# Grouped-query attention on one core: Q pieces copied four times by GpSimd for full-width transposes, and Q loaded by another pattern

## The chip, the cores and the metric

The kernel runs on one core of one Trainium2 chip. The metric is the device time of one execution in microseconds (us), as a median over several runs; the profile is of one more execution. The core has five engines with instruction streams of their own: PE (TensorE: matmuls and, on a second row of the profile called PEld, the loading of their weights), DVE (VectorE), ACT (ScalarE), POOL (GpSimd) and SP (SyncE, which here only issues DMAs). Sixteen DMA engines move data between HBM and the on-chip memory SBUF. PE writes its results to another on-chip memory, PSUM, in which DVE and ACT read them.

## The reference

```python
B, Hq, Hkv, Sq, Sk, D = 16, 32, 8, 16, 2048, 128      # all bf16
k = jnp.repeat(k, rep, axis=1)                         # rep = Hq // Hkv = 4
v = jnp.repeat(v, rep, axis=1)
scores = jnp.einsum("bhqd,bhkd->bhqk", q, k) * D ** -0.5
p = softmax(scores, axis=-1)
out = jnp.einsum("bhqk,bhkd->bhqd", p, v)
```

There are 16 x 8 = 128 groups (one batch, one KV head). A group has 4 x 16 = 64 rows of Q, and 2048 x 128 of K and of V, 512 KB each. K and V together are 134 MB; Q and the output are 2.1 MB each.

## The kernel before, in words

**Tiling.** Two groups make a *pair*: 128 rows of Q, and so 128 rows of scores. There are 64 pairs, p = 0 to 63. K and V of a pair are loaded whole (1 MB each; six buffers Kn, eight buffers Vb). Eight pairs make a *chunk* c of Q: 1024 rows, 256 KB, loaded at once into Qn (two buffers), eight rows side by side in each of 128 partitions.

**One pair.** DVE transposes K in blocks of 32x32 four-byte words, two bf16 at a time (line 261, Kn to KT). Since a word holds two neighbouring elements of D and only 32 words fit in a block's side, the head dimension of 128 falls into four pieces of 32 (numbered by b and e), and the keys into four strips of 32 partitions. S (line 217): 32 matmuls, 4 pieces x 4 strips x 2 groups, each with 32 rows contracted, add the scores up in PSUM. DVE scales and negates them and keeps the minimum (line 277, Sneg). ACT takes the exponential and the row sums (line 306, P). PE transposes P in two halves of four 128x128 blocks (line 232, "PT"), and ACT moves each half to SBUF (line 316, "pe"). PV (line 243): 32 matmuls with V into O_ps. ACT scales by the reciprocal of the row sum (line 326, "norm"), and SP stores the 32 KB of the pair (line 166).

**Q.** S needs Q transposed: for each of the four pieces, 32 elements of D on the partitions, and the same 32 again on each of the four strips of 32 partitions. A *part* (c, i), i = 2b + e, makes one piece for the 1024 rows of a chunk. At line 200 PE transposes, for each of the 8 rows j of a partition, the 32 columns of the piece (every second element of 64) four times, once into each strip r: 32 transposes a part, 32 parts in all. ACT then moves the part, 128x1024, from PSUM to QT (line 296), with j taken innermost, so that the rows come out in their order.

**Order.** The order on PE and on ACT is written out by hand in two lists. First the four parts of chunk 0 and S(0). Then for each p: PE has S(p+1), a part of the next chunk if p mod 8 is 2 to 5, PT(p) in two halves, PV(p); ACT has exp(p), norm(p-1), the part's move, the two halves. PE's transposes go through three stages of PSUM in turn, and each waits until ACT has emptied its stage. DVE has Sneg(p), the reciprocal of p-1 and the two K transposes of p+2.

**SP's queue.** For t = 0, 1, ...: load K(t); load a chunk c of Q where t = max(0, 8c-7); load V(t-3); store pair t-7. Each waits in that one queue: K for DVE's transposes of the buffer's last user, V for PV of its last user (line 152), a store for the norm of its pair (line 165), and from chunk 2 on Q for the transposes of the chunk two before (line 159). Every load adds 16 to its semaphore, one from each of the 16 DMA engines, and its reader waits for all 16.

**GpSimd** makes the two identity matrices for the transposes (lines 132 to 135) and nothing else.

Of the kernel before, what the change touches and what calls it, by code (L numbers as in the profile page):

```python
# [5 lines left out]
ACT = mybir.ActivationFunctionType  # L6
ALU = mybir.AluOpType
BF16 = mybir.dt.bfloat16
# [8 lines left out]
NQ = 2  # L17
# [6 lines left out]
def bass_standalone__gqa_softmax__sampling_kernel(  # L24
# [14 lines left out]
    NQC = NP // 8  # L39
# [3 lines left out]
    sb = lambda name, shape, dt: ctx.enter_context(nc.sbuf_tensor(name, shape, dt))  # L43
    sem = lambda name: ctx.enter_context(nc.semaphore(name))

    iota_t = sb("iota_t", [128, 128], I32)
    ident = sb("ident", [128, 128], BF16)
# [5 lines left out]

    KT = [sb(f"KT{i}", [128, 2, J * 64], F32) for i in range(NKT)]
    Qn = [sb(f"Qn{i}", [128, 8, 128], BF16) for i in range(NQ)]

    QT = [sb(f"QT{i}", [128, 4, 1024], BF16) for i in range(2)]
    Sneg = [sb(f"Sneg{i}", [128, Sk], F32) for i in range(2)]
    P = [sb(f"P{i}", [128, Sk // 2], F32) for i in range(2)]
# [14 lines left out]
    sem_q = [sem(f"sem_q{i}") for i in range(NQ)]  # L74
    sem_o = [sem(f"sem_o{i}") for i in range(NO)]
    sem_kt = sem("sem_kt")
    sem_max = sem("sem_max")
    sem_rec = sem("sem_rec")
    sem_s = sem("sem_s")
    sem_st = sem("sem_st")  # L80
# [5 lines left out]
    qf = q.rearrange("b h s d -> (b h s) d")  # L86
# [8 lines left out]
    def stage(*what):  # L95
        stages.append(what)
        return len(stages) - 1
# [9 lines left out]
    for p in range(NP):  # L107
# [5 lines left out]
        c, i = divmod(p, 8)  # L113
        if c + 1 < NQC and 2 <= i < 6:
            q_part(c + 1, i - 2)
        for h in range(2):
            u = stage("P", p, h)
# [4 lines left out]
    last_q = {what[1:]: u for u, what in enumerate(stages) if what[0] == "Q"}  # L122
    last_p = {what[1:]: u for u, what in enumerate(stages) if what[0] == "P"}

    def stage_ap(u):
        return ST_ps[:, 512 * (u % NSTAGE):512 * (u % NSTAGE + 1)]

    with nc.Block() as block:

        @block.gpsimd  # L130
        def _(gp):
            gp.iota(iota_t[:, :], [[1, 128]], base=0, channel_multiplier=-1).then_inc(sem_id, 1)  # L132
            gp.wait_ge(sem_id, 1)
            gp.tensor_scalar(ident[:, :], iota_t[:, :], 0.0, None, op0=ALU.is_equal).then_inc(sem_id, 1)  # L134
            gp.tensor_scalar(ident4[:, :], iota_t[:, :], 0.0, None, op0=ALU.is_equal).then_inc(sem_id, 1)  # L135

        @block.sync
        def _(sp):
            def load_k(p):
                s = p % NK  # L140
                if p >= NK:
                    sp.wait_ge(sem_kt, 2 * (p - NK) + 2)
                if p == 0:
                    for g in range(2):
                        sp.dma_start(Kn[s][:, g, :], kf[:, g, :]).then_inc(sem_k0[g], 16)  # L145
                else:
                    sp.dma_start(Kn[s][:, :, :], kf[:, 2 * p:2 * p + 2, :]).then_inc(sem_k[s], 16)

            def load_v(p):
                s = p % NV  # L150
                if p >= NV:
                    sp.wait_ge(sem_pv, p - NV + 1)
                dst = Vb[s][:, :, :, :].rearrange("a g j d -> a g (j d)")
                sp.dma_start(dst, vf[:, 2 * p:2 * p + 2, :]).then_inc(sem_v[s], 16)

            def load_q(c):
                s = c % NQ
                if c >= NQ:
                    sp.wait_ge(sem_st, last_q[c - NQ, 3] + 1)
                src = qf[1024 * c:1024 * (c + 1), :].rearrange("(a j) d -> a j d", j=8)  # L160
                sp.dma_start(Qn[s][:, :, :], src).then_inc(sem_q[s], 16)

            def store(p):
                s = p % NO
                sp.wait_ge(sem_nm, p + 1)
                sp.dma_start(of[128 * p:128 * (p + 1), :], Osb[s][:, :]).then_inc(sem_o[s], 16)

            for t in range(NP + SLAG + 1):
                if t < NP:
                    load_k(t)  # L170
                for c in range(NQC):
                    if t == max(0, 8 * c - QLEAD):
                        load_q(c)
                if 0 <= t - VLAG < NP:
                    load_v(t - VLAG)
                if 0 <= t - SLAG < NP:
                    store(t - SLAG)
            for s in range(NO):
                sp.wait_ge(sem_o[s], 16 * (NP // NO))

        @block.tensor
        def _(pe):
            pe.wait_ge(sem_id, 3)

            def free(u):
                if u >= NSTAGE:
                    pe.wait_ge(sem_ev, u - NSTAGE + 1)

            for op in pe_prog:
                if op[0] == "QT":  # L190
                    _, c, i, u = op
                    if i == 0:
                        pe.wait_ge(sem_q[c % NQ], 16 * (c // NQ + 1))
                    free(u)
                    dst = stage_ap(u).bitcast(BF16)
                    src = Qn[c % NQ][:, :, :].rearrange("p j (b c e) -> p j b e c", b=2, e=2)
                    b, e = divmod(i, 2)
                    for j in range(8):
                        for r in range(4):
                            ins = pe.transpose(dst[32 * r:32 * (r + 1), 128 * j:128 * (j + 1)], src[:, j, b, e, :], ident[:, :])  # L200
                    ins.then_inc(sem_st, 1)
                elif op[0] == "S":
                    _, p = op
                    pe.wait_ge(sem_kt, 2 * p + 2)
                    if p >= 1:
                        pe.wait_ge(sem_max, p)
                    c, i = divmod(p, 8)
                    if i == 0:
                        pe.wait_ge(sem_ev, last_q[c, 3] + 1)
                    kt = KT[p % NKT][:, :, :].bitcast(BF16).rearrange("p g (t b x e) -> p g b e t x", t=J // 2, b=2, e=2)  # L210
                    qt = QT[c % 2]
                    for acc in range(4):
                        b, e = divmod(acc, 2)
                        for r in range(4):
                            rows = slice(32 * r, 32 * (r + 1))
                            for g in range(2):
                                ins = pe.matmul(  # L217
                                    S_ps[64 * g:64 * (g + 1), 512 * r:512 * (r + 1)],
                                    qt[rows, acc, 128 * i + 64 * g:128 * i + 64 * (g + 1)],
                                    kt[rows, g, b, e, :, :],  # L220
                                    start=(acc == 0), stop=(acc == 3),
                                )
                    ins.then_inc(sem_s, 1)
                elif op[0] == "PT":
                    _, p, h, u = op
                    if h == 0:
                        pe.wait_ge(sem_exp, p + 1)
                    free(u)
                    dst = stage_ap(u)
                    for t in range(4):  # L230
                        x = 4 * h + t
                        ins = pe.transpose(dst[:, 128 * t:128 * (t + 1)], P[p % 2][:, 128 * x:128 * (x + 1)], ident4[:, :])  # L232
                    ins.then_inc(sem_st, 1)
                elif op[0] == "PV":
                    _, p = op
                    pe.wait_ge(sem_ev, last_p[p, 1] + 1)
                    pe.wait_ge(sem_v[p % NV], 16 * (p // NV + 1))
                    if p >= 1:
                        pe.wait_ge(sem_nm, p)
                    pt = PT[p % NPT][:, :, :].bitcast(BF16).rearrange("p t (q e) -> p t e q", e=2)  # L240
                    for j in range(J):
                        for g in range(2):
                            ins = pe.matmul(  # L243
                                O_ps[64 * g:64 * (g + 1), 0:128],
                                pt[:, j // 2, j % 2, 64 * g:64 * (g + 1)],
                                Vb[p % NV][:, g, j, :],
                                start=(j == 0), stop=(j == J - 1),
                                skip_group_check=True,
                            )
                    ins.then_inc(sem_pv, 1)  # L250
# [38 lines left out]
        def _(act):  # L289
            for op in act_prog:  # L290
                if op[0] == "qe":
                    _, c, i, u = op
                    act.wait_ge(sem_st, u + 1)
                    if c >= 2 and i == 0:
                        act.wait_ge(sem_s, 8 * (c - 1))
                    act.activation(  # L296
                        QT[c % 2][:, i, :].rearrange("p (a j) -> p a j", j=8),
                        stage_ap(u).bitcast(BF16).rearrange("p (j a) -> p a j", j=8), ACT.Copy,
                    ).then_inc(sem_ev, 1)
                elif op[0] == "exp":  # L300
                    _, p = op
# [9 lines left out]
                elif op[0] == "pe":  # L311
                    _, p, h, u = op
# [7 lines left out]
                else:  # L320
                    _, p = op
# [34 lines left out]
```

## Time and profile before

| | us |
|---|---|
| median of 3 runs (lowest, highest) | 357.61 (357.51, 357.91) |
| span of the profiled execution, first to last instruction | 357.7 |
| PE busy, of that line 200 (Q transposes) | 248.2, 22.9 |
| DVE busy, of that lines 277 and 261 | 296.1, 146.1 and 150.7 |
| ACT busy, of that line 296 (Q part to QT), x32 | 249.4, 32.4 |
| POOL busy | 1.4 |
| loads of V, K: median from issue to landing | 16.0, 15.0 |
| loads of Q, x8: median from issue to landing | 14.3 |

How to read it: the profiled execution's own time is known by its span, 357.7 us. Times of the profile are counted from the span's start. A line of a group of instructions gives the busy time and the mean of one; matmuls overlap, so that the mean of one can be many times the distance between two. A line of the waits gives the engine, what it was about to do and what ended its waiting, then us in total, how many times, and the longest. A line of the timeline gives the start, the length, the engine, the source line, what was done, and in brackets the idle time before it. GpSimd's few instructions are: MEMSET of one column 98 to 101 ns, IOTA of 128 columns (int32) 234 ns, TENSOR_SCALAR of 128 columns (int32 to bf16, to f32) 534 and 526 ns.

The queues: q1 carries what SP issues, q8 and q14 carry instructions to the engines. The packets of q1 are 4 KB for K and V, 2 KB for Q and 256 bytes for the output.

### The profile page before, as it was taken

How to read it: one execution, taken by the hardware profiler on the slowest of the kernel's cores; microseconds unless marked ns; L12 is line 12 of the kernel's file. 1: busy time of each engine (PE TensorE's matmuls, PEld its weight loads, DVE VectorE, ACT ScalarE, POOL GpSimd, SP SyncE). 2: the span in 40 equal slices, each digit the busy share in tenths (PEclk: the TensorE clock that was granted, in tenths of full speed). 3: DMA queues.
4: the chain of work that ended last, by engine and by line, in shares of the span. 5: the costliest groups of instructions: out<-in, count | busy, mean ns of one | idle time of the engine just before them, and what ended most of it. 6: DMA issues, size and time to landing. Idle time of an engine off the chain costs nothing.

```text
span 357.7 us, 12753 instructions
## 1 busy us (share of the span) xinstructions
PE 248.2 (69%) x5632; PEld 171.7 (48%) x5632; DVE 296.1 (83%) x320; ACT 249.4 (70%) x353; POOL 1.4 (0%) x7
## 2 busy tenths in 40 slices
PE   2587786686776587776677775776766777667675
PEld 2355554454444364454444554454544555444444
DVE  2879979979699839998798699699778889996880
ACT  3469867778478568788676588478676688765674
POOL 1000000000000000000000000000000000000000
PEclk9769989999899969999998899899889899998898
DMA  7999999999999999999999999999999999999930
GB/s 292 414 408 408 410 407 408 411 412 412 410 412 409 410 412 407 412 413 408 409 411 412 411 407 410 411 411 413 409 409 412 401 409 410 410 411 404 377 139 7
DMA packets 45253, 139.22 MB, mean 389 GB/s; under 512 B 11408, under 2 KB 11408, under 8 KB 45200
## 3 DMA queue, kind: packets, MB, share of 16 engines
q1 hardware_dynamic: 45200, 138.42, 97.4%
q8 instruction: 44, 0.72, 0.8%
q14 instruction: 9, 0.07, 0.1%
HBM read 136.31 MB, written 2.10 MB: 387 GB/s over the span
## 4 chain that ended last, share of the span: by engine, by line
PE 51%; issue 26%; ACT 17%; DVE 3%; DMA 1%; SPq 0%; DVEq 0%; ACTq 0%
PE O_ps L243 20%; PE S_ps L217 18%; ACT PT L316 14%; PE ST_ps L232 8%; PE ST_ps L200 5%; DVE KT L261 2%; ACT QT L296 2%; DMA Qn<-in_q_dram 1%; ACT P L306 1%; DVE Sneg L277 1%; SPq L145 0%; ACT O L326 0%; DVE rrec L268 0%; DVEq L276 0%; ACTq L315 0%
## 5 line engine op out<-in xcount | busy, mean ns | idle before, releaser
L277 DVE TENSOR_SCALAR_CACHE_REDUCE Sneg<-S_ps 128x2048 f32<-128x2048 f32 x64 | 146.1, 2283 | 46.1 <-PE S_ps L217 45.7
L261 DVE STREAM_TRANSPOSE KT<-Kn 128x1024 f32<-128x1024 f32 x128 | 150.7, 1216 | 6.9 <-DMA Kn<-in_k_dram 6.9
L306 ACT ACTIVATE P<-Sneg,nbias 128x2048 bf16<-128x2048 f32 x64 | 128.4, 2006 | 24.1 <-DVE Sneg L277 24.1
L243 PE MATMUL O_ps<-Vb,PT 128*64 128x128 bf16 x2048 | 76.3, 230 | 84.3 <-ACT PT L316 55.4
L243 PEld LDWEIGHTS O_ps<-Vb,PT 128*64 128x64 bf16 x2048 | 65.6, 116 | 100.3 <-ACT PT L316 68.0
L316 ACT ACTIVATE PT<-ST_ps 128x512 f32<-128x512 f32 x128 | 70.1, 596 | 38.8 <-PE ST_ps L232 38.8
L217 PE MATMUL S_ps<-KT,QT 32*64 32x512 bf16 x2048 | 82.5, 432 | 6.1 <-DVE Sneg L277 2.5
L232 PE MATMUL ST_ps<-ident,P 128*128 128x128 f32 x512 | 76.3, 296 | 6.5 <-ACT P L306 6.2
L232 PEld LDWEIGHTS ST_ps<-ident,P 128*128 128x128 f32 x512 | 60.4, 151 | 28.7 <-ACT P L306 18.0
L296 ACT ACTIVATE QT<-ST_ps 128x1024 bf16<-128x1024 bf16 x32 | 32.4, 1023 | 36.0 <-PE ST_ps L200 35.8
L217 PEld LDWEIGHTS S_ps<-KT,QT 32*64 32x64 bf16 x2048 | 28.5, 110 | 30.3 <-issue 13.4
L200 PE MATMUL ST_ps<-ident,Qn 128*32 128x128 bf16 x1024 | 22.9, 239 | 10.0 <-DMA Qn<-in_q_dram 6.4
L200 PEld LDWEIGHTS ST_ps<-ident,Qn 128*32 128x32 bf16 x1024 | 17.2, 106 | 23.9 <-issue 23.8
L326 ACT ACTIVATE O<-O_ps,rrec 128x128 bf16<-128x128 f32 x64 | 23.0, 360 | 6.4 <-PE O_ps L243 6.2
L306 ACT ACTIVATION_READ_ACCUMULATOR P<-Sneg,nbias 128x1 f32 x64 | 12.5, 195 | 0.0
L268 DVE RECIPROCAL rrec<-rowsum 128x1 f32<-128x1 f32 x64 | 10.1, 158 | 2.1 <-ACT P L306 2.1
L277 DVE DVE_READ_ACCUMULATOR Sneg<-S_ps 128x1 f32 x64 | 5.3, 82 | 0.0
L296 ACT ACT_TABLE_LOAD x1 | 1.3, 1283 | 0.7 <-PEq L341 0.7
L134 POOL TENSOR_SCALAR ident<-iota_t 128x128 bf16<-128x128 int32 x1 | 0.5, 534 | 0.1
L135 POOL TENSOR_SCALAR ident<-iota_t 128x128 f32<-128x128 int32 x1 | 0.5, 526 | 0.0
L132 POOL IOTA iota_t<- 128x128 int32 x1 | 0.2, 234 | 0.4 <-POOLq L341 0.4
L341 POOL MEMSET const-bfloat16-1.0<- 128x1 bf16 x1 | 0.1, 101 | 0.0
(3 smaller groups left out, 0.3 us busy)
## 6 DMA issues: line engine op xcount, KB each, us to landing
Vb<-in_v_dram SPq DMA_DIRECT2D x64, 1024.0 KB, 16.0
Kn<-in_k_dram SPq DMA_DIRECT2D x63, 1024.0 KB, 15.0
Qn<-in_q_dram SPq DMA_DIRECT2D x8, 256.0 KB, 14.3
out_dram<-O SPq DMA_DIRECT2D x64, 32.0 KB, 13.9
Kn<-in_k_dram SPq DMA_DIRECT2D x2, 512.0 KB, 3.9
```

Of the source, the lines that this page charges most:

```text
L134: gp.tensor_scalar(ident[:, :], iota_t[:, :], 0.0, None, op0=ALU.is_equal).then_inc(sem_id, 1)
L200: ins = pe.transpose(dst[32 * r:32 * (r + 1), 128 * j:128 * (j + 1)], src[:, j, b, e, :], ident[:, :])
L217: ins = pe.matmul(S_ps[64 * g:64 * (g + 1), 512 * r:512 * (r + 1)], qt[rows, acc, 128 * i + 64 * g:128 * i + 64 * (g + 1)], kt[rows, g, b, ...
L232: ins = pe.transpose(dst[:, 128 * t:128 * (t + 1)], P[p % 2][:, 128 * x:128 * (x + 1)], ident4[:, :])
L243: ins = pe.matmul(O_ps[64 * g:64 * (g + 1), 0:128], pt[:, j // 2, j % 2, 64 * g:64 * (g + 1)], Vb[p % NV][:, g, j, :], start=(j == 0), sto ...
L261: dve.transpose(KT[p % NKT][:, g, :].rearrange("p (t b a e) -> p t e b a", t=J // 2, b=2, e=2), Kn[p % NK][:, g, :].bitcast(F32).rearrange ...
L268: dve.reciprocal(rrec[:, p:p + 1], rowsum[:, p:p + 1]).then_inc(sem_rec, 1)
L277: dve.tensor_scalar(Sneg[p % 2][:, :], S_ps[:, :], -scale, None, op0=ALU.mult, op1=ALU.min, accum_out=nbias[:, p:p + 1],).then_inc(sem_max, 1)
L296: act.activation(QT[c % 2][:, i, :].rearrange("p (a j) -> p a j", j=8), stage_ap(u).bitcast(BF16).rearrange("p (j a) -> p a j", j=8), ACT. ...
L306: act.activation(P[p % 2][:, :].bitcast(BF16).rearrange("p (t r x) -> p t r x", t=8, r=4), Sneg[p % 2][:, :].rearrange("p (r t x) -> p t r ...
L316: act.activation(PT[p % NPT][:, 4 * h:4 * (h + 1), :].rearrange("p t q -> p (t q)"), stage_ap(u), ACT.Copy,).then_inc(sem_ev, 1)
L326: act.activation(Osb[p % NO][:, :], O_ps[:, 0:128], ACT.Copy, scale=rrec[:, p:p + 1]).then_inc(sem_nm, 1)
```

## The change

GpSimd lays the two 64-column halves of every Q row, for a whole chunk, four times side by side in a new buffer Q4 (one copy instruction a chunk, 4096 elements in each partition). PE transposes 128 columns of Q4 at a time, four copies of the same 32 columns, so that one transpose fills the four strips: 8 transposes a part for 32. PE now waits for the copy and not for the load; the copy waits for the load and for the last transposes of the chunk before, and SP's load of chunk c waits for the copy of chunk c-2. The load of Q places rows differently: partition 16x + y holds the eight rows from row 64y + 8x on, by a source pattern [8, 16, 1024] that was [128, 8, 128]. ACT's read from PSUM undoes this order.

```diff
+    Q4 = sb("Q4", [128, 8, 2, 4, 64], BF16)
...
+    sem_q4 = sem("sem_q4")
...
             gp.tensor_scalar(ident4[:, :], iota_t[:, :], 0.0, None, op0=ALU.is_equal).then_inc(sem_id, 1)
+            for c in range(NQC):
+                gp.wait_ge(sem_q[c % NQ], 16 * (c // NQ + 1))
+                if c >= 1:
+                    gp.wait_ge(sem_st, last_q[c - 1, 3] + 1)
+                src = Qn[c % NQ][:, :, :].rearrange("p j (b x) -> p (j b) x", b=2)
+                gp.tensor_copy(
+                    Q4[:, :, :, :, :].rearrange("p j b r x -> p (j b) r x"),
+                    src.unsqueeze(2).to_broadcast([128, 16, 4, 64]),
+                ).then_inc(sem_q4, 1)
...
                 if c >= NQ:
-                    sp.wait_ge(sem_st, last_q[c - NQ, 3] + 1)
-                src = qf[1024 * c:1024 * (c + 1), :].rearrange("(a j) d -> a j d", j=8)
+                    sp.wait_ge(sem_q4, c - NQ + 1)
+                src = qf[1024 * c:1024 * (c + 1), :].rearrange("(y x j) d -> x y (j d)", x=8, j=8)
                 sp.dma_start(Qn[s][:, :, :], src).then_inc(sem_q[s], 16)
...
                     if i == 0:
-                        pe.wait_ge(sem_q[c % NQ], 16 * (c // NQ + 1))
+                        pe.wait_ge(sem_q4, c + 1)
...
-                    src = Qn[c % NQ][:, :, :].rearrange("p j (b c e) -> p j b e c", b=2, e=2)
+                    src = Q4[:, :, :, :, :].rearrange("p j b r (c e) -> p j b e (r c)", e=2)
                     b, e = divmod(i, 2)
                     for j in range(8):
-                        for r in range(4):
-                            ins = pe.transpose(dst[32 * r:32 * (r + 1), 128 * j:128 * (j + 1)], src[:, j, b, e, :], ident[:, :])
+                        ins = pe.transpose(dst[:, 128 * j:128 * (j + 1)], src[:, j, b, e, :], ident[:, :])
...
                     act.activation(
-                        QT[c % 2][:, i, :].rearrange("p (a j) -> p a j", j=8),
-                        stage_ap(u).bitcast(BF16).rearrange("p (j a) -> p a j", j=8), ACT.Copy,
+                        QT[c % 2][:, i, :].rearrange("p (y x j) -> p y x j", x=8, j=8),
+                        stage_ap(u).bitcast(BF16).rearrange("p (j x y) -> p y x j", j=8, x=8), ACT.Copy,
                     ).then_inc(sem_ev, 1)
```

## The prediction

> **What bounds the kernel now.** I read the page first. Parts 1 to 3, cut to the lines that carry it:
>
> ```profile
> PE 248.2 (69%) x5632; PEld 171.7 (48%) x5632; DVE 296.1 (83%) x320; ACT 249.4 (70%) x353; POOL 1.4 (0%) x7
> ...
> DMA  7999999999999999999999999999999999999930
> GB/s 292 414 408 408 410 407 408 411 412 412 410 412 409 410 412 407 412 413 408 409 411 412 411 407 410 411 411 413 409 409 412 401 409 410 410 411 404 377 139 7
> ...
> q1 hardware_dynamic: 45200, 138.42, 97.4%
> q8 instruction: 44, 0.72, 0.8%
> ```
>
> No compute engine is full; the sixteen DMA engines are, from the second slice to the 37th, at a flat 410 GB/s. The chain view says otherwise (PE 51%, issue 26%), so I went to the waits, and from them to the last stretch in order of time. In the waits, "issue" means that the profile names no releaser:
>
> ```profile
> PE O_ps L243 <- ACT PT L316: 55.4, 52, 1.7
> PE O_ps L243 <- issue: 28.8, 17, 3.1
> ```
>
> ```profile
> 332.57 1.08 ACT L316 ACTIVATE PT<-ST_ps 128x512 f32<-128x512 f32 x2 [0.49 <-PE ST_ps L232]
> ...
> 334.32 1.92 PE L243 MATMUL O_ps<-Vb,PT 128*64 128x128 bf16 x32 [1.35 <-ACT PT L316]
> ```
>
> ACT ends at 333.65, yet PE starts PV(59) only at 334.32. Line 243 also waits for V. The trace records when each of a load's 16 completion marks arrives (each load adds 16, one per DMA engine). V(59)'s last mark is at 334.23, 0.09 us before PV(59). I paired all 64: from pair 7 on, PV(p) starts exactly 0.09 us after V(p)'s last mark in 32 of 53 pairs up to p=59, and otherwise ACT is just behind. So V's landing sets the pace (5.2 us a pair); compute, when behind, runs 4.55 to 4.65 us a pair (after a PE stall at pair 20 the 3.7 us were made good by pair 25). After PV(59) the last V's are early, and a fixed tail of four compute-paced pairs ends the span: 357.7 - 334.3 = 23.4 us. **The end is V(59)'s last mark plus 23.4 us.**
>
> The marks of one load, in us after its first one:
>
> ```
> V(3)   first  32.09: 0 0 .1 .1 .1 .1 .1 .3 .3 .4 .4 .5 .8 1.9 2.0 2.3
> V(27)  first 157.48: 0 0 .1 .4 .5 1.1 2.0 2.0 3.0 3.1 3.5 3.6 4.0 5.1 5.2 5.5
> V(59)  first 324.87: 0 .2 .2 .4 .5 .6 2.3 3.0 6.6 6.7 7.2 7.3 7.4 7.9 8.9 9.4
> ```
>
> So the engines are not equal: six early, two between, eight late. The late eight carry the instruction fetches: 3 of them precede V(3), where three marks stand out; 41 precede V(59), where the late eight are 59 us behind in sum, **1.44 us a fetch**. 44 fetches of 16 KB match PE's 11,264 matmuls and weight loads (256 each). A late engine cannot speed up when others rest: its 4 KB packets take 159 ns in mid-run and 159 ns at 344 to 347, with eight engines idle.
>
> **The change, step by step.**
>
> *PE transposes (line 200).* Removed 24 of 32 in each of 32 parts. Today 32 narrow ones in four column groups take 0.63 to 0.80 us a part together (22 ns each, not the row's 239 ns, which overlap). Eight full-width ones: by line 243, whose 32 matmuls in two column groups last 1.09 us, 68 ns each, 0.54 us; by line 232 (eight f32 transposes in 1.09 us) 1.09 us. I take 0.54, as bf16 is nearer. Between -0.2 and +0.4 us a part, 32 parts; all of it lies ahead of a PV that waits for V. Cost and gain on the path: nothing. Without that cover it would be -6 to +13 us. The new wait of PE for the copy has S, PT and PV queued behind it; it is bare in the first part only (below).
>
> *Instruction fetches.* 768 transposes with their weight loads are 1,536 instructions, 6 of 44 blocks. 6 x 1.44 / 8 late engines = **-1.1 us** at V(59) (0 to -2.9, as whole fetches fall on single engines).
>
> *ACT eviction (line 296).* Same 1,024 columns, source still strided: the row's 1.02 us stays. The new order of reads is in no row: bounds -0.2 to +1.0 a part, the same cover; bare it would be -6 to +32 us.
>
> *GpSimd copy.* 8 copies of 4,096 bf16 per partition. Bounds: IOTA's 128 columns less a one-column MEMSET, (234 - 101)/127 = 1.05 ns each, so 4.4 us; TENSOR_SCALAR whole, 534/128 = 4.2 ns, so 17.1 us. Nearest is TENSOR_SCALAR, which reads and writes, by its slope (534 - 101)/127 = 3.4 ns: 14 us, likely too much for a plain copy. [...] Nothing but the next copy is queued on GpSimd. The copy for c >= 1 starts when part 3 of c-1 is transposed and has five pairs, 26 us, before its own transposes. The first lies bare: Q lands at 6.25, S(0) is at 11.40, so everything starts 4 to 17 us later. What is queued behind it: SP reaches the first store at 22.80 and finds the norm done at 22.05; later it blocks there. But loads take 15 to 16 us from issue to landing, so DMA stays busy to about 38 us, and the start may slip some 14 us before an engine runs dry. Compute then regains up to 0.6 us a pair. Cost: nothing; at 17.1 us about +3. SP's wait for the third Q moves to an earlier event. If GpSimd held up DVE: DVE idles 17%, 7 us in eight pairs, which hides a copy up to 7 us.
>
> *Q load.* The same 256 KB in 2 KB packets: 1,024 packets, so 8 per engine and load now, from a pattern whose outermost count is 128. Now the outermost count is 8. The trace shows no such load. Bounds: still sixteen engines, 0; eight engines with 16 packets each, so eight more at 84.5 ns (the packet records), 0.68 us a load, 8 loads: +5.4 us on those, -5.4 us on the rest; fewer engines still would be worse. What this does to V(59)'s last mark depends on which engines: +5.4 if even one of the latest is among them. I take +5.4: 128 is divided evenly over sixteen and 8 cannot be, and any set of eight misses all late engines only if it is exactly the other eight.
>
> [...]
>
> Sum: 357.7 + 5.4 - 1.1 = 362.0 by the profiled execution, whose span stands 0.1 us above the median of 357.61. **Forecast 361.9 us.** Its own range, from the fetch bounds and 10% on top of the load: 357.6 + 5.4 - 2.9 = 360.1 to 357.6 + 5.9 = 363.5.
>
> **Rivals.**
> 1. *The eight engines are the early ones* (ends faster). Then at V(59) the two between stand at 3.0 + 5.4 = 8.4, the early at 6.0, the late at 9.4 - 5.4 - 1.1 = 2.9; last mark 9.4 to 8.4: -1.0, **356.6 us**. It decides only if no late engine carries Q. For it: that six and two are just eight. Against: one split of many, and nothing in the profile says so.
> 2. *The load still uses sixteen engines*, or the split does not follow the outermost count: only the fetches go, -1.1, **356.5 us**.
> 3. *The start drains the queue*: a first copy near 17 us, with the Q term: **365 us**. For: the TENSOR_SCALAR row; against: a copy is lighter.
> 4. *PE is the bound*, as the chain's 5% for line 200 suggests: 32 x 0.2 = -6, 351.5 us. Against: the 0.09 us after V.
>
> **How the numbers follow.** Forecast 0.62, rival 1 0.17, rival 2 0.14, rival 3 0.05, rival 4 0.02. Under 0.2% (0.7 us, about what a measurement of this kernel can tell from no change) fall about a quarter of rivals 1 and 2. Slower 0.66, within 0.08, faster 0.26. Forecast's own range holds some 0.55, so the range that holds 8 in 10 must reach to rivals 1 and 2: 356.0 to 363.5.
>
> **What would show it.** Right: Qn's marks come from eight engines (8 at once, 8 with the data) with 16 packets each; V(59)'s last mark some 4 us later, near 338.5, first mark of the early eight earlier; 38 fetch packets; PV still 0.09 us behind V; line 200 near 0.55 us a part with no effect. Wrong: Qn's packets on all engines; PV no longer behind V (GpSimd or DVE ends last); a DMA slice well under 400 GB/s near 30 us (rival 3); or late marks pulled in (rival 1).

## The result

The changed kernel takes 371.94 us (median of 4 runs, 371.47 to 372.41) against 357.76 us for the kernel before, measured beside it: ratio 1.0387, 95% interval 1.0363 to 1.0411. Slower was forecast, but by 1.2% and not by 3.9%; the forecast's range ended at 363.5 us. The profiled execution has a span of 370.5 us.

### The profile page after: what moved, and what is told of

It is laid out like the page before. It is cut to its first block, busy times and chain, and to the rows that moved or that the text cites. A ratio compares the mean times of both kernels' runs of the same rounds, so it can differ in the third digit from the quotient of the medians.

```text
span 370.5 us, 11232 instructions
## 1 busy us (share of the span) xinstructions
PE 244.1 (66%) x4864; PEld 171.3 (46%) x4864; DVE 296.1 (80%) x320; ACT 248.7 (67%) x353; POOL 30.3 (8%) x15
## 2 busy tenths in 40 slices
DMA packets 45183, 139.12 MB, mean 376 GB/s; under 512 B 11344, under 2 KB 11344, under 8 KB 45136
## 3 DMA queue, kind: packets, MB, share of 16 engines
q1 hardware_dynamic: 45136, 138.42, 97.6%
## 4 chain that ended last, share of the span: by engine, by line
PE 57%; ACT 20%; issue 18%; DMA 2%; POOL 1%; DVE 1%; SPq 0%; ACTq 0%; DVEq 0%
PE O_ps L252 21%; PE S_ps L226 18%; ACT PT L325 17%; PE ST_ps L241 15%; PE ST_ps L209 4%; DMA Qn<-in_q_dram 2%; ACT P L315 1%; ACT QT L305 1%; POOL Q L142 1%; DVE Sneg L286 1%; SPq L155 0%; ACT O L335 0%; ACTq L313 0%; ACTq L324 0%; DVEq L285 0%
## 5 line engine op out<-in xcount | busy, mean ns | idle before, releaser
L252 PE MATMUL O_ps<-Vb,PT 128*64 128x128 bf16 x2048 | 77.4, 233 | 102.5 <-ACT PT L325 56.9
L252 PEld LDWEIGHTS O_ps<-Vb,PT 128*64 128x64 bf16 x2048 | 67.2, 118 | 117.5 <-ACT PT L325 68.5
L241 PE MATMUL ST_ps<-ident,P 128*128 128x128 f32 x512 | 74.5, 293 | 5.9 <-ACT P L315 5.6
L305 ACT ACTIVATE QT<-ST_ps 128x1024 bf16<-128x1024 bf16 x32 | 32.4, 1024 | 34.5 <-PE ST_ps L209 34.5
L142 POOL COPY Q<-Qn 128x4096 bf16<-128x4096 bf16 x8 | 28.8, 3600 | 249.5 <-DMA Qn<-in_q_dram 245.7
L209 PE MATMUL ST_ps<-ident,Q 128*128 128x128 bf16 x256 | 21.5, 235 | 11.4 <-POOL Q L142 11.4
L209 PEld LDWEIGHTS ST_ps<-ident,Q 128*128 128x128 bf16 x256 | 16.3, 106 | 24.6 <-issue 24.6
```

What stands on the lines that cost most here:

```text
L142: gp.tensor_copy(Q4[:, :, :, :, :].rearrange("p j b r x -> p (j b) r x"), src.unsqueeze(2).to_broadcast([128, 16, 4, 64]),).then_inc(sem_q ...
L209: ins = pe.transpose(dst[:, 128 * j:128 * (j + 1)], src[:, j, b, e, :], ident[:, :])
L252: ins = pe.matmul(O_ps[64 * g:64 * (g + 1), 0:128], pt[:, j // 2, j % 2, 64 * g:64 * (g + 1)], Vb[p % NV][:, g, j, :], start=(j == 0), sto ...
L305: act.activation(QT[c % 2][:, i, :].rearrange("p (y x j) -> p y x j", x=8, j=8), stage_ap(u).bitcast(BF16).rearrange("p (j x y) -> p y x j ...
```

## The profile after

The lines of the page that answer to those shown of before (busy time; DMA share and bandwidth in 40 slices; the queues), and two groups:

```profile
PE 244.1 (66%) x4864; PEld 171.3 (46%) x4864; DVE 296.1 (80%) x320; ACT 248.7 (67%) x353; POOL 30.3 (8%) x15
...
DMA  7999999999999999999999999999999999999930
GB/s 268 352 409 408 409 350 410 411 412 400 353 413 410 412 368 388 411 409 404 322 395 412 411 409 330 397 404 406 406 315 411 411 414 384 411 412 410 406 146 11
...
q1 hardware_dynamic: 45136, 138.42, 97.6%
q8 instruction: 38, 0.62, 0.7%
...
L142 POOL COPY Q<-Qn 128x4096 bf16<-128x4096 bf16 x8 | 28.8, 3600 | 249.5 <-DMA Qn<-in_q_dram 245.7
...
L209 PE MATMUL ST_ps<-ident,Q 128*128 128x128 bf16 x256 | 21.5, 235 | 11.4 <-POOL Q L142 11.4
```

The share row has not changed: every slice between the first and the last two is still a 9. The bandwidth row has: where one of the eight loads of Q runs, a slice or two falls from about 410 GB/s to between 315 and 400. Engines that are busy throughout and move less have slower packets, as the packet records below show. So the share of busy time hides this loss, and the row of GB/s shows it.

V still sets the pace. The last of the sixteen marks of V(59), read here as one from each of the 16 DMA engines when its share of the load has landed (the packet records of before hold 3,216 marks for 201 transfers, 16 each), comes at 347.55 (334.23 before). The timeline has PV(59) 0.09 us behind it, 1.3 us after ACT has finished at 346.32:

```profile
345.24 1.08 ACT L325 ACTIVATE PT<-ST_ps 128x512 f32<-128x512 f32 x2 [0.82 <-PE ST_ps L241]
...
347.64 1.08 PE L252 MATMUL O_ps<-Vb,PT 128*64 128x128 bf16 x32 [2.00 <-issue]
```

In 37 of the 53 pairs from 7 to 59 PV starts 0.09 us behind V (32 before). After V(59)'s last mark 22.9 us are left (23.5 before). The span grew by 12.8 us: the mark came 13.3 us later, and what follows it took 0.6 us less.

The transposes that the change is named for gained almost nothing. One part before, in 32 narrow transposes, and one after, in 8 full-width ones:

```profile
27.32 0.63 PE L200 MATMUL ST_ps<-ident,Qn 128*32 128x128 bf16 x32
...
33.32 0.62 PE L209 MATMUL ST_ps<-ident,Q 128*128 128x128 bf16 x8
```

Over the 32 parts the median is 0.63 us before and 0.62 us after. A quarter of the instructions took nearly the same time, so PE had little to gain from the change.

The third load of Q, cut out by windows (columns: stretch, its length, busy time of the engines, PE clock, DMA share, GB/s), first before, then after:

```profile
40.00:44.40 4.40, 3.69 (x104) 2.52 (x98) 3.80 (x3) 3.40 (x6) 0.00 (x0) 1.00 1.03 411
44.40:47.50 3.10, 1.85 (x52) 1.37 (x60) 2.67 (x5) 2.81 (x5) 0.00 (x0) 0.98 1.04 406
```

```profile
40.00:47.60 7.60, 5.58 (x142) 3.93 (x144) 7.60 (x10) 7.18 (x11) 0.00 (x0) 1.00 1.03 412
47.60:50.30 2.70, 1.89 (x26) 1.26 (x16) 2.25 (x2) 1.82 (x4) 0.00 (x0) 1.00 1.08 255
```

While Q is loaded, 406 GB/s have become 255, with the DMA engines as busy as ever. The packet records of the same stretch say what is slow: Q's 2 KB packets take 148 ns on average (84 before), and the 4 KB packets of K and V between them about 262 ns (164 before). In the five later loads the 4 KB packets take 208 to 233 ns. Over the whole run the packet time, as a mean over the sixteen engines, rose by 2.5 us for Q (5.5 to 8.1) and by 10.3 us for K and V (331.7 to 342.1). Together that is 12.9 us, close to the 13.3 us of V(59). Four fifths of it is in packets that the change did not touch.

Q's semaphore shows the split. The first load has one mark at 2.77, right after its issue, and then eight marks from 6.64 to 7.61; since its reader waits for 16, the early mark must bring the other 8. Before, there were sixteen marks, from 5.64 to 6.25. Over the whole run q1 has 45,136 packets for 45,200, eight marks fewer in each of the eight loads.

## The experiments

Theory A: the load alone costs the time. Its rival B: the compute side does (copy, later start, eviction). Within A there are three candidates: scattered HBM rows, eight engines, or the way the partitions are divided among engines. Q rows that come out permuted or wrong, where the expectations say so and in experiment 7, change no amount of work. "Q packet" is the mean time of one 2 KB packet over all eight loads; the kernel before has 86 ns. Each ratio is against the kernel before in runs beside it. Experiments 1 and 3 to 8 edit the kernel before; from 3 on the new line stands in place of the one that experiment 1 removes.

**1. The load alone, on the kernel before.**

```diff
-                src = qf[1024 * c:1024 * (c + 1), :].rearrange("(a j) d -> a j d", j=8)
+                src = qf[1024 * c:1024 * (c + 1), :].rearrange("(y x j) d -> x y (j d)", x=8, j=8)
```

> The kernel before with the new Q load pattern and nothing else; the 1024 Q rows of a chunk come out permuted within the chunk (the eviction does not undo the new order), the work is the same. Theory A (the load does it: Q on eight DMA engines, which slows all packets while it runs): about 372 to 373 us, since the six instruction fetches are not saved, with V(59) landing 13 to 15 us later and dips to some 350 GB/s in the page's bandwidth row. Theory B (the compute side does it: GpSimd copy, later start, ACT order): within 1 us of 357.7. My prediction's own price for the load, 0.68 us each, would give 363.

Measured: 375.85 us, ratio 1.0473 (1.0421 to 1.0526), above the 372 to 373 us expected. V(59)'s last mark is at 351.37, 17.1 us later than before, Q packet 126 ns. The page's bandwidth row has the same dips, with no GpSimd copy in the kernel:

```profile
GB/s 249 341 407 409 410 347 409 411 410 401 346 411 414 411 363 377 404 393 412 340 398 410 409 385 333 404 406 409 383 356 365 400 413 410 410 412 398 388 126 7
```

So the load alone costs all of it, and some 3 us more than the whole change does. The compute side's gain (experiment 2) is about 1 us of that; the rest stays open.

**2. The compute side alone: the changed kernel with the old load and the old eviction order.**

```diff
-                src = qf[1024 * c:1024 * (c + 1), :].rearrange("(y x j) d -> x y (j d)", x=8, j=8)
+                src = qf[1024 * c:1024 * (c + 1), :].rearrange("(a j) d -> a j d", j=8)
...
-                        QT[c % 2][:, i, :].rearrange("p (y x j) -> p y x j", x=8, j=8),
-                        stage_ap(u).bitcast(BF16).rearrange("p (j x y) -> p y x j", j=8, x=8), ACT.Copy,
+                        QT[c % 2][:, i, :].rearrange("p (a j) -> p a j", j=8),
+                        stage_ap(u).bitcast(BF16).rearrange("p (j a) -> p a j", j=8), ACT.Copy,
```

> The changed kernel with the old Q load (outermost 128) and the old eviction order; GpSimd copy and full-width transposes stay. Theory A: 356 to 357.5 us (the six fetches saved, up to 1.1 us, and the later start hidden). Theory B: about 371 us. If the late start costs by itself (first norm some 5 us later), 358 to 362.

Measured: 357.94 us, ratio 0.9973 (0.9933 to 1.0012), with the GpSimd copies in the kernel and no dips in the bandwidth row:

```profile
GB/s 296 414 409 408 409 407 411 410 410 411 409 410 411 413 407 411 411 411 409 410 412 412 410 410 409 408 412 412 409 411 413 411 413 410 408 412 412 385 146 7
```

B is out, and a small gain stays possible. The same kernel again, in more runs:

> The changed kernel with the old Q load and the old eviction order once more, for a narrower interval: the compute half of the change alone. By the fetch term (six of 44 instruction blocks less, 1.1 us at V(59)) 356.5 to 357.5 us, a ratio of 0.996 to 0.999; without it 1.000; if the later start costs, over 1.000.

Measured: 357.48 us against 358.42, ratio 0.9972 (0.9954 to 0.9991). The copies, the wider transposes and the later start together cost nothing and bring some 0.3%. V(59)'s last mark is at 332.8, 1.5 us earlier than in the profile of before, with 39 fetch packets for 44. But V(59)'s first mark is 0.6 us earlier too (324.24 for 324.87), on engines that by the prediction carry no fetches. So that the fetches bring the gain is not shown.

**3. The same outermost count, HBM rows in the old order.**

```diff
+                src = qf[1024 * c:1024 * (c + 1), :].rearrange("(x y j) d -> x y (j d)", x=8, j=8)
```

> The kernel before with the Q load written as 8 x 16 x 1024 but in the old order: every partition gets what it got before, and each of the eight outer indices is one stretch of 32 KB in HBM. Theory A1 (eight engines and where they write): as e1, 371 to 373 us, with 8 marks per Q load instead of 16. Theory A2 (the scattered rows in HBM, 2 KB pieces of one 16 KB stretch read by eight engines at once): near my old price, 361 to 364 us, by double work of eight engines alone. If the two outer dimensions are merged again before the chip sees them, 16 marks and 357.7 us.

Measured: 357.85 us, ratio 0.998 (0.9943 to 1.0017), 16 marks, which fits the last case of the expectation, two dimensions that are one again before the chip sees them. It tells nothing of A, only that this contiguous pattern costs nothing in the new spelling either.

**4. Interleaved rows over sixteen engines.**

```diff
+                src = qf[1024 * c:1024 * (c + 1), :].rearrange("(y x j) d -> x y (j d)", x=16, j=8)
```

> The kernel before with the new kind of pattern but outermost count 16 (16 x 8 x 1024): rows of HBM interleaved as in the change, now over sixteen outer indices; Q rows come out permuted within the chunk. Theory A1 (eight engines): 16 marks, within 1 us of 357.7. Theory A2 (interleaved rows in HBM): 365 us or more. If it is where an engine writes (each outer index is a block of neighbouring partitions rather than the even spread of 128), something between, 360 to 368 us, with 16 marks but slow packets during Q.

Measured: 366.38 us, ratio 1.0226 (1.0182 to 1.0269), 16 marks, Q packet 116 ns. Sixteen engines and still slow: the doubled work of eight engines, my only price, cannot be all.

**5. Scattered rows, outermost count 128.**

```diff
+                src = qf.rearrange("(a n j) d -> n a (j d)", a=128, n=8, j=8)[c]
```

> The kernel before with the source of Q at an even stride of 16 KB from partition to partition, outermost count 128 (the load of chunk c takes every eighth piece of 2 KB of the whole of Q; Q rows come out permuted over chunks). Sixteen engines, the same spread over partitions as before, but HBM rows as far apart as in the change. If scattered rows in HBM make the packets slow (what the interleaved load over sixteen engines left open at 366.4): 365 us or more, Q packets over 105 ns. If it is where and by how many engines the partitions are written: within 1 us of before, Q packets near 85 ns.

Measured: 358.0 us, ratio 0.9994 (0.9971 to 1.0017), Q packet 88 ns. Scattered rows in HBM alone are not the cause.

**6 and 7. HBM in order, eight and sixteen outer indices kept apart by gaps.**

```diff
+                src = qf[1008 * c:1008 * c + 1088, :].rearrange("(x y j) d -> x y (j d)", x=8, j=8)[:, 0:16, :]
```

```diff
+                src = qf[1000 * c:1000 * c + 1152, :].rearrange("(x y j) d -> x y (j d)", x=16, j=8)[:, 0:8, :]
```

> The kernel before with Q loaded as 8 x 16 x 1024 from eight stretches of 32 KB that leave 2 KB between them, so that the two outer dimensions cannot be merged (chunks overlap a little, so some Q rows are wrong ones; the work is the same). [...] If the writing is the cause: 372 to 377 us as with the change's load, Q packets near 126 ns, 8 marks. If scattered rows are the cause and eight engines add only their own double work: 358 to 363 us, Q packets near 85 ns; above 361 the late engines are among the eight, below 358 they are not.

> [...] If the writing in blocks of partitions is the cause of the 8 us of the interleaved load over sixteen engines: 364 to 368 us, Q packets near 110 ns. If scattered HBM rows are: within 1 us of before.

Measured: eight 372.35 us, ratio 1.0416 (1.0344 to 1.0487), Q packet 120 ns, 45,136 packets on q1 and so eight marks a load; sixteen 367.32 us, ratio 1.0247 (1.0183 to 1.0311), Q packet 112 ns, 45,200 packets and so sixteen marks. Without any interleaving both are as slow as the interleaved loads, within the intervals. The windows of the third Q load with sixteen:

```profile
40.00:45.60 5.60, 3.90 (x104) 2.72 (x104) 4.85 (x9) 4.44 (x8) 0.00 (x0) 1.00 1.03 410
45.60:49.80 4.20, 3.56 (x72) 2.33 (x72) 3.16 (x3) 2.73 (x5) 0.00 (x0) 1.00 1.02 300
```

**8. Two outer dimensions cut finer: 32 x 4 and 64 x 2.**

```diff
+                src = qf[984 * c:984 * c + 1280, :].rearrange("(x y j) d -> x y (j d)", x=32, j=8)[:, 0:4, :]
```

```diff
+                src = qf[944 * c:944 * c + 1536, :].rearrange("(x y j) d -> x y (j d)", x=64, j=8)[:, 0:2, :]
```

> The kernel before with Q loaded as 32 x 4 x 1024 from stretches of 8 KB that leave 2 KB between them (some Q rows are wrong ones; the work is the same). [...] If each engine still gets one run of 8 neighbouring partitions: as with sixteen stretches, 365 to 369 us, Q packets 105 to 118 ns. If the outer indices are dealt out over the engines, so that blocks shrink to 4 partitions: clearly less, 358 to 363 us, Q packets below 100 ns.

> The same with 64 x 2 x 1024, stretches of 4 KB that leave 2 KB between them. If any pattern with two outer dimensions costs this, whatever its outermost count: again 365 to 369 us. If the outermost count decides, so that a finer cut comes nearer to the single dimension of 128: less than with 32, down to 357 to 360 us.

Measured: 32 gives 358.68 us, ratio 1.0027 (1.0004 to 1.0050); 64 gives 357.86 us, ratio 1.0003 (0.9986 to 1.0019). From the second load on, Q packets take 84 to 89 ns, as before; the first load's are slower (135 and 117 ns), which brings the means of all eight to 91 and 90 ns. The ladder, all with gaps between the stretches:

```
outermost count     8       16       32       64      128 (before)
time, us          372.35  367.32   358.68   357.86   357.74 to 358.20
V(59) last mark   348.30  343.25   334.03   334.65   334.23
```

It is not the second dimension, which 32 and 64 have too (0.3% and nothing): it is an outermost count of 8 or 16 (4.2% and 2.5%), by which each outer index of the load is a block of 16 or 8 neighbouring partitions. The stretches in HBM get shorter along the ladder too, but they do not decide: a count of 16 is slow with interleaved rows (experiment 4) and with 16 KB stretches (7), and a count of 128 is fast with scattered rows (5) and with contiguous ones.

**9. The forms alone, with nothing else in flight.** Before the kernel's own work SP loads 256 KB eight times, into a tile that nobody reads, each after the last has landed. `alone` is the list of the four forms: the old one, the change's, sixteen stretches with gaps, eight stretches with gaps.

```diff
+            for n, src in enumerate(alone + alone):
+                sp.dma_start(Qx[:, :, :], src).then_inc(sem_x, 16)
+                sp.wait_ge(sem_x, 16 * (n + 1))
```

> The kernel before with eight extra Q loads of 256 KB at the very start, one at a time with nothing else in flight, into a tile that nobody reads: twice the four forms (old; the change's 8 x 16; sixteen stretches with gaps; eight stretches with gaps). Theory crowding with K and V: alone, each form's packets take about 84 ns, the old form and the sixteen stretches finish alike, the forms over eight engines take 0.7 us longer. Theory self-collision (the engines of one such load hinder each other): packets of 110 to 130 ns in the new forms even alone. The rest of the kernel runs as before, later by the time of the eight loads, some 20 us.

Measured (386.32 us, one run, of which 28 before the first K load): every form's packets have a median of 84 ns. Their means are 99 to 130 ns, but they do not follow the forms' cost in the kernel: 109 and 118 ns for the old form, 99 and 100 for the change's, 130 and 120 for sixteen stretches, 102 and 107 for eight. From first to last packet the old form takes 1.26 and 1.30 us, sixteen stretches 1.45 and 1.40, the change's form 2.17 and 2.01, eight stretches 2.02 and 2.05. Eight engines cost 0.6 to 0.9 us, as I had priced them, **when nothing else moves**. In these runs the change's form has slower packets than the old form only beside K and V (148 ns for 84 in the third load).

**10. V one step earlier in SP's order.** The end is V(59)'s mark plus a compute-paced tail, so an earlier V should bring an earlier end. The kernel of experiment 2, and:

```diff
-VLAG = 3
+VLAG = 2
```

> The changed kernel with the old Q load and old eviction order, and V loaded one step earlier in SP's order (VLAG 2 for 3). It tests the sum end = last mark of the binding V plus a compute-paced tail. By it every V but the last two lands one 1 MB load, 2.5 us, earlier; the binding pair becomes V(61), and the end comes 2 to 3 us before that of the kernel with VLAG 3: 354 to 356 us. If the end were set by compute or by the last byte alone: no change, 357 to 358.

Measured: 356.30 us against 358.20, ratio 0.9952 (0.9934 to 0.9969): 0.5% faster than the kernel before, and so faster than both kernels, but just short of the 354 to 356 us expected. V(59) lands at 330.5, some 2.2 us earlier than with VLAG 3, but PV(59) starts 1.0 us behind it: only 2 of the 53 pairs still start 0.09 us behind V, so compute has become the last to arrive, and less came out than expected. The gain over VLAG 3 (0.9972) lies within the two intervals.

## Why the prediction was wrong

Right were the bound (PV waits for V, 0.09 us behind, with a tail of 23.5 us before and 22.9 after, where the prediction's 23.4 counts from PV(59)'s start), so that the chain's PE share meant nothing; the PE term (0.62 us a part for 0.54 forecast, on nobody's path); the GpSimd copy's cover (3.6 us, below both bounds; S(0) came 5.0 us later, and from pair 7 on PV was behind V again); and eight marks for Q. The whole compute side brought 0.9 us (experiment 2, second set of runs), near the -1.1 us of the fetch term, but that it came from the fetches is not shown. The sign was right too, though the term behind it was only about a third of what the load cost.

**The step that failed is the price of the Q load**, "eight engines with 16 packets each, so eight more at 84.5 ns", +5.4 us. The count of engines was right, the 84.5 ns were not. I took a packet's time as its engine's own, because 4 KB packets took 159 ns both in mid-run and with eight engines idle. That shows that idle neighbours do not help. It does not show that neighbours cannot hurt, and all loads of the old trace had an outermost count of 128, so none could show it. The term measured 14.8 to 15.1 us at V(59)'s last mark (347.55 against 332.77 and 332.49 in the two profiles of the changed kernel with the old load and the old eviction order), and 17.1 us on the kernel before (experiment 1). In parts, from the loads with gaps: sixteen engines cost 9.1 us (367.32 - 358.20), which I had at nothing; going to eight adds 5.0 us more (372.35 - 367.32). That this is close to my 5.4 is partly luck: between these two profiles the mean packet time per engine rose by 2.9 us as well (7.2 to 7.7 for Q, 339.7 to 342.1 for K and V). With the price fell the upper bound: I wrote that only fewer engines would be worse, though an operation that is in no row may also slow what runs beside it.

Two expectations of mine fell with the same step. The early marks did not come earlier: V(59)'s first one went from 324.87 to 339.78, so the eight engines that carry no Q came later too. And the question of my first rival, whether the late engines carry Q, lost its weight; which engines fetch instructions, and whether the fetches make eight of them late, stays open.

What is shown: the cost goes with the outermost count (8, 16 against 32, 64, 128), not with HBM order nor with the number of engines alone, and the change's packets were slower than the old form's only beside K and V (148 ns for 84 in the third load; alone 99 and 100 for 109 and 118). How a low count slows them is not shown. That each engine then writes a block of neighbouring partitions, as the expectations of experiments 4, 7 and 8 suppose, is my conjecture: no run here shows which engine wrote which partition, nor what the slow packets of K and V waited for.

## What to carry to other kernels

In a kernel that DMA bounds, look at a load's access pattern as closely as at its bytes: keep the outermost count at 128 (here 8 cost 4.2%, 16 2.5%, 32 0.3% and 64 nothing), and put a reordering of rows into an engine's read, not into the load; ACT's move of a part took 1.02 us in either order. Price a new transfer by what it does to the transfers beside it, too, and watch GB/s, since the busy share of the DMA engines stayed at its full value here (1.04 before, 1.08 after) while 406 GB/s became 255. Before working on an engine, check whether its waits end with a load's last mark, even where the profile names another releaser.

## What the runs showed of the hardware that was not expected

- A 256 KB load whose outermost count is 8 took the 4 KB packets of other loads in flight from 164 to about 262 ns, and the core from 406 to 255 GB/s, while the third of its eight runs lasted; alone, its own packets had a median of 84 ns, as ever.
- Sixteen engines are not enough: with an outermost count of 16 all sixteen marks come from data, and the kernel is still 2.3 to 2.5% slower (experiments 4 and 7).
- Eight transposes over the full width of PE (0.62 us) took nearly as long as 32 narrow ones of 32 columns (0.63 us).
- GpSimd copied 4,096 bf16 per partition, each source half read four times, in 3,600 ns: 0.88 ns an element, a quarter of the 3.4 ns of the slope from its one-column MEMSET to its 128-column TENSOR_SCALAR.
